# Attention and maxout layer on one Trainium2 core: four units of seven tiles become units of 7, 8, 7 and 6

## The chip, the cores and the metric

The kernel runs on one core of a Trainium2 chip. The metric is the device time of one execution in microseconds; the number given for a kernel is the median of its runs.

## The reference

What is computed, cut to the arithmetic (8 x 8 heads of 576 positions and 64 features, in chunks of 64; the token matrix x is 4608 x 512, d_ff is 768):

```python
scores = scale * np.matmul(q_c, k_c.transpose(0, 1, 2, 4, 3))
scores = scores - np.max(scores, axis=-1, keepdims=True)
attn = np.exp(scores)
attn = attn / (np.sum(attn, axis=-1, keepdims=True) + 1e-09)
out = np.matmul(attn, v_c)
...
x = np.ascontiguousarray(attn_out.transpose(0, 2, 1, 3)).reshape(B * S, H * D)
h = np.maximum(np.maximum(x @ w1, x @ w2), x @ w3)
return (h @ w_out).astype(np.float32)
```

## The kernel before

The 36 tiles of 128 tokens are worked in two groups of four tiles (`GROUPS`) and then in four units of seven (`UNITS`, line 27). For each tile the attention comes first: scores S (L221), the softmax on VectorE, ScalarE and GpSimd (L226 to L188), four transposes T (L244), the values V (L256), and a copy into x. For a group or a unit the hidden layer follows, then the projection with w_out.

Every 32-bit operand is held as a high and a low part, and `three` (L170 to L173) makes of each product three matmuls: low by high, high by low, high by high. In the text a matmul of such a three is called a product.

In the groups the hidden layer is a plain one over 512 tokens. In a unit it is a scheme with seven products for a 2 x 2 block product: the tokens of the unit are two halves of `count * 64` columns (`half`, L404), the d_model is split in two, and pairs of d_ff blocks form the two outputs. `operands` (L434) makes the seven moving operands X1 to X7 from the unit's x in `stage`, as sums and differences of its four blocks. The seven stationary operands, sums and differences of weights, are made once by `store` (L351), written to DRAM and loaded again for each set through a ring of two places (`load`, L440): 768 KB by L443 and 1024 KB by L447. A set is a pair of d_ff blocks and one of w1, w2, w3. There are nine sets in a unit, each with seven products in the order `ORDER = (1, 6, 5, 7, 2, 3, 4)`, each of two halves of the contraction and three matmuls: 42 matmuls a set, 378 a unit, all `half` columns wide. After set n, `load` is planned for set n + 2, into the ring's place that set n has left. Results go from one of five PSUM banks by copies (L471), sums (L474, L477) and GpSimd's sums (L480, L483) into `kept` and `most`, and the maximum over the three weights (L486) is split into the high and low part H (L492, L496). The projection (L521) of a unit runs after its nine sets, 18 matmuls of 512 columns a tile, and its outputs are copied (L518) and stored (L519) through four buffers.

The order on every engine is written out. For the first group it is the string `FIRST`; after it a planner walks through the TensorE steps, keeps a clock `now` by the tabled step times `STEP` (a three with 512 columns) and `STEP_H` (a three of a unit), and puts every other operation into the program when its due time has come. The attention of unit u + 1 is laid into unit u by `tiles` (L689): a *cluster* of V of one tile, S of the tile two further on and T of the next, at equal distances over the time that the caller gives. All of it runs on one stream of TensorE, so a cluster stands between products. Unit 0's tiles are made during the second group; unit 1's from the second group's projection through unit 0's hidden layer; unit 2's from unit 0's projection through unit 1's hidden layer, and so on. The last unit has no attention beside it.

The buffers: `HALF` (line 28) is the width for which `stage`, `kept`, `most` and H are made; X is made 512 wide and cut to `HALF`. `H_AT` (L627) lists the places of the twelve H buffers, six of a pool that the groups used, five of a late pool, one of the attention's.

Of the kernel before, what the change touches and what calls it, by code (L numbers as in the profile page):

```python
# [10 lines left out]
F32R = mybir.dt.float32r  # L11
# [9 lines left out]
P = 128  # L21
NT = B * S // P
DM, DF, DO = 512, 768, 512
CT, JT = DM // P, DF // P
SCALE = 1.0 / float(D) ** 0.5
GROUPS = [4, 4]
UNITS = [7] * 4
HALF = 448
STEP, TILE = 0.6815, 1.55
STEP_H = 0.6003  # L30
ORDER = (1, 6, 5, 7, 2, 3, 4)
SOFTMAX = (("mx", 1.0), ("sub", 1.9), ("exp", 2.8), ("sum", 3.8), ("eps", 4.7), ("rec", 4.9), ("nrm", 5.3))
ON_PE = {"V": 0.6, "S": 0.6, "T": 0.35}
# [29 lines left out]
def chunk_attn_maxout_kernel(  # L63
# [16 lines left out]
    att = ctx.enter_context(tc.tile_pool(name="att", bufs=1))  # L80
# [6 lines left out]
    hpool = ctx.enter_context(tc.tile_pool(name="hpool", bufs=1))  # L87
# [23 lines left out]
    for name in FIRST.split():  # L111
        k = (3 * int(name[1]) + int(name[2])) if name[0] in "WAXY" else None
# [235 lines left out]
    sets = [(jp, w) for jp in range(JT // 2) for w in range(3)]  # L348
# [52 lines left out]
    def unit(t0, count, rooms):  # L401


        half = count * 64  # L404
        X, ring = {}, {}
        hh, hl = [None] * JT, [None] * JT
        stage, m, s = rooms["stage"], rooms["m"], rooms["s"]
# [6 lines left out]
            return lambda: stage()[:, 2 * k:2 * k + 2, c * half:(c + 1) * half]  # L414

        def room(n):
            return lambda: s()[:, 2 * n:2 * n + 2]

        b11, b21, b12, b22 = (block(k, c) for c in range(2) for k in range(2))
        source = {1: b11, 2: b21, 3: b22, 4: room(0), 5: room(0), 6: room(1), 7: b12}  # L420
# [3 lines left out]

        def high(i):
            def fn():
                X[i] = rooms["X"](i)
                nc.scalar.copy(out=X[i][:, 0], in_=source[i]())
            return fn

# [28 lines left out]
        def hidden(n):  # L459
            jp, w = sets[n]  # L460
            a, b = 2 * jp, 2 * jp + 1
            o = {}

            def M(j, c):
                return m()[:, j - a, c, :half]

            def kept(k):
                return s()[:, k, :half]

            def copy(i, k):  # L470
                return lambda: nc.scalar.copy(out=kept(k), in_=o[i])  # L471

            def sum_to(k, i, q):
                return lambda: nc.vector.tensor_tensor(out=kept(k), in0=o[i], in1=kept(q), op=plus)  # L474

            def value(i, k, j, c):
                return lambda: nc.vector.tensor_tensor(out=o[i] if w else M(j, c), in0=o[i], in1=kept(k), op=plus)  # L477

            def third():
                nc.gpsimd.tensor_tensor(out=kept(2), in0=kept(2), in1=kept(1), op=plus)  # L480

            def fourth():
                nc.gpsimd.tensor_tensor(out=kept(1) if w else M(b, 1), in0=kept(1), in1=kept(3), op=plus)  # L483

            def greater(j, c, of):
                return lambda: nc.vector.tensor_tensor(out=M(j, c), in0=of(), in1=M(j, c), op=most)  # L486

            def high(j, c):
                def fn():
                    if hh[j] is None:  # L490
                        hh[j], hl[j] = (rooms["H"](2 * j + k) for k in range(2))
                    nc.scalar.copy(out=hh[j][:, c * half:(c + 1) * half], in_=M(j, c))  # L492
                return fn

            def low(j, c):
                return lambda: nc.vector.tensor_tensor(out=hl[j][:, c * half:(c + 1) * half], in0=M(j, c),  # L496
                                                       in1=hh[j][:, c * half:(c + 1) * half].bitcast(F32), op=minus)

            def most_of(at, j, c, of):
                ops = [(at, greater(j, c, of))] if w else []  # L500
                return ops + ([(at + 1.4, high(j, c)), (at + 2.3, low(j, c))] if w == 2 else [])

            after = {1: [(0.25, copy(1, 0))], 6: [(0.25, sum_to(2, 6, 0))], 5: [(0.25, copy(5, 1))],
                     7: [(0.25, sum_to(3, 7, 2)), (1.0, third), (2.2, fourth)],
                     2: [(0.25, value(2, 0, a, 0))] + most_of(0.8, a, 0, lambda: o[2]),
                     3: [(0.25, value(3, 2, a, 1))] + most_of(0.8, a, 1, lambda: o[3]),
                     4: [(0.25, value(4, 3, b, 0))] + most_of(0.8, b, 0, lambda: o[4]) + most_of(1.4, b, 1, lambda: kept(1))}
            for i in ORDER:
                o[i] = bank()[:, :half]
                for k in range(2):  # L510
                    hi, lo = weights(n, i, k)
                    three(o[i], hi, lo, X[i][:, 0, k, :half], X[i][:, 1, k, :half], k == 0, k == 1)
                    yield STEP_H, after[i] if k else []

        def output(tt, of):
            outputs.append(tt)
# [28 lines left out]
    def hold(name, make):  # L545
        if name not in held:
            held[name] = make()
        return held[name]

    def stage():  # L550
        return hold("stage", lambda: stage_p.tile([P, CT, 2 * HALF], F32, name="stage"))

# [71 lines left out]

    order = []
    late = {}
    H_AT = [(hpool, f"h{k}") for k in range(6)] + [("late", f"k{k}") for k in range(5)] + [(att, "aa")]  # L627

    def H(k):
        pool, tag = H_AT[k]  # L630
        return (late["hold"] if pool == "late" else pool).tile([P, 2 * HALF], F32R, name="H", tag=tag, bufs=1)

    def X(i):
        return hold(("X", i), lambda: late["hold"].tile([P, 2, 2, 512], F32R, name=f"X{i}")[:, :, :, :HALF])

    rooms = dict(
        stage=stage, X=X, H=H,
        m=lambda: hold("m", lambda: late["hold"].tile([P, 2, 2, HALF], F32, name="most")),
        s=lambda: hold("s", lambda: late["hold"].tile([P, 4, HALF], F32, name="kept")),
        ring=lambda n, k: late["hold"].tile([P, (6, 8)[k], 256], F32R, name="ring", tag=f"r{n % 2}{k}"))  # L640

    places = []
    groups, parts = [g0], []
    g = moe(starts[1], lambda: x_tiles(1))
    groups.append(g)
    units, t0 = [], sum(GROUPS)
    for count in UNITS:
        units.append((unit(t0, count, rooms), t0, count))
# [4 lines left out]
    def steps(n):  # L653
        if n not in steps_of:
            t0 = sum(GROUPS)
            first = t0 + n // UNITS[0] * UNITS[0]
            steps_of[n] = begun[t0 + n] if t0 + n in begun else plain_steps(t0 + n, stage, (t0 + n - first) * P)
        return steps_of[n]

    tiles_in_units = sum(UNITS)  # L660

# [13 lines left out]
    def first_tiles(time):  # L675
        gap = (time - 8.0) / 8
        for n in range(UNITS[0] + 2):
            at = now + 7.0 + gap * n
            insert(at, (("V", n - 2), ("S", n)))
            softmax(n, at, nc.vector if n < UNITS[0] else nc.gpsimd)  # L680
            if n < UNITS[0] + 1:
                insert(at + 9.2, (("T", n),))
# [6 lines left out]
    def tiles(u, time):  # L689
        if u >= len(units):  # L690
            return
        lead = 10.9
        gap = (time - 10.0 - lead) / (UNITS[u] - 1)
        for k in range(UNITS[u]):
            n, at = sum(UNITS[:u]) + k, now + lead + gap * k
            insert(at, (("V", n), ("S", n + 2), ("T", n + 1)))
            softmax(n + 2, at, nc.gpsimd)
            plan(at - 16.0, 0.0, lambda n=n: steps(n)["v"]())
            plan(at + 1.0, 0.0, lambda n=n: steps(n)["x"]())
            if n + 1 < tiles_in_units:  # L700
                plan(at + 0.9, 0.0, lambda n=n: steps(n + 1)["at"]())
# [16 lines left out]
    def load(u, n, *at):  # L718
        if n >= len(sets):
            u, n = u + 1, n - len(sets)  # L720
        if u < len(units):
            for t, fn in zip(at, units[u][0]["load"](n)):
                plan(now + t, 0.0, fn)

    inner = 3 * JT * CT * STEP + 7 * TILE
    span = len(sets) * 14 * STEP_H + 6 * TILE
    parts += [("do", lambda: first_tiles(inner - 2.0))]
    parts += [("steps", lambda j=j, w=w: g["hidden"](j, w)) for j in range(JT) for w in range(3)]
    parts += [("do", change), ("do", lambda: operands(0)),
              ("do", lambda: tiles(1, 4 * JT * STEP + span)), ("do", lambda: load(0, 0, 0.0, 1.0)), ("do", lambda: load(0, 1, 2.0, 3.0))]  # L730
    parts += [("steps", lambda: g["project"](0, 1)), ("steps", lambda: g["project"](2)), ("steps", lambda: g["project"](3))]
    for u, (it, t0, count) in enumerate(units):
        for n in range(len(sets)):
            parts.append(("steps", lambda it=it, n=n: it["hidden"](n)))
            parts.append(("do", lambda u=u, n=n: load(u, n + 2, 0.3, 0.9)))
        parts.append(("do", lambda u=u: operands(u + 1)))
        parts.append(("do", lambda u=u, count=count: tiles(u + 2, count * JT * STEP + span + TILE)))
        parts += [("steps", lambda it=it: it["project"](0, 1, 2, before=4))]
        parts += [("steps", lambda it=it, tt=tt: it["project"](tt)) for tt in range(3, count)]
    now = -10.0  # L740
# [8 lines left out]
    with tc.manual_schedule(engines={ET.PE, ET.DVE, ET.Activation, ET.Pool, ET.SP}):  # L749
        first_group()  # L750
        for what, make in parts:
# [3 lines left out]
            for after in make():  # L755
                step, after = after if isinstance(after, tuple) else (STEP, after)
# [36 lines left out]
```

## Time and profile before

| | |
|---|---|
| median of 3 runs | 639.48 us (639.41 to 639.81) |
| the profiled execution | 639.17 us |
| its span in the profile | 637.4 us |
| TensorE busy | 628.0 us |
| VectorE, ScalarE, GpSimd busy | 410.7, 232.7, 214.5 us |
| products of the units, 448 columns | 1512, in four times 378 |
| HBM traffic | 209 GB/s over the span |

The span runs from the first to the last instruction of the program. A row of the timeline has the start, the duration (of merged rows: to the last one's end), the engine, the line, the operation, what it writes and reads, and its size. Durations of TensorE's rows overlap, as matmuls are pipelined; what counts there is the distance between starts. "PE" is TensorE, "PEld" its weight loads, "DVE" VectorE, "ACT" ScalarE, "POOL" GpSimd, "SP" SyncE, which issues the DMAs.

### The profile page before, as it was taken

What the parts mean: (1) busy time and instruction counts of PE and PEld (TensorE: products, weight loads), DVE (VectorE), ACT (ScalarE), POOL (GpSimd) and SP (SyncE); (2) the same over time, 40 slices, a digit from 0 to 9 for tenths busy, and PEclk for the clock granted to TensorE, in tenths of its full rate; (3) what the DMA queues carried; (4) which work ended last, traced back from release to release, by engine and by line L of the source; (5) the groups of instructions that cost most, each with busy time, mean ns of one, the idle gap of its engine ahead of it and who ended that gap; (6) DMA issues with size and microseconds to landing.
All of it is one profiled execution on the core that took longest, in us unless ns stands there. A gap on an engine that the chain in (4) does not pass through costs nothing.

```text
span 637.4 us, 12371 instructions
## 1 busy us (share of the span) xinstructions
PE 628.0 (99%) x5101; PEld 540.8 (85%) x5102; DVE 410.7 (64%) x661; ACT 232.7 (37%) x400; POOL 214.5 (34%) x185
## 2 busy tenths in 40 slices
PE   7899999999999999999999999999999999999997
PEld 3888878878889998888999998898998889999986
DVE  4889854788856676891675769337584842756520
ACT  4888633454532322452132325322331431212121
POOL 2423577765423233231323334023322421222200
PEclk9999999999999999999999999999999999999999
DMA  8988559576846656273466527537563523555211
GB/s 328 358 298 305 184 183 356 212 243 231 316 159 270 248 207 273 79 286 133 173 274 238 220 105 281 198 124 256 216 225 139 214 100 117 201 197 217 111 50 66
DMA packets 35911, 133.70 MB, mean 210 GB/s; under 512 B 3984, under 2 KB 6288, under 8 KB 30096
## 3 DMA queue, kind: packets, MB, share of 16 engines
q1 hardware_dynamic: 35856, 132.92, 56.5%
q8 instruction: 40, 0.66, 0.4%
q14 instruction: 15, 0.12, 0.1%
HBM read 106.95 MB, written 25.95 MB: 209 GB/s over the span
## 4 chain that ended last, share of the span: by engine, by line
PE 91%; DVE 5%; ACT 2%; issue 1%; DVEq 0%; ACTq 0%
PE pm L171 28%; PE pm L172 28%; PE pm L173 28%; PE s L256 3%; PE tp L244 2%; PE s L221 2%; DVE e L231 1%; PE pm L583 1%; DVE mx L226 1%; DVE sm L179 1%; DVE s L382 1%; ACT e L235 1%; DVE sm L182 1%; DVE xl L267 0%; DVE m L307 0%
## 5 line engine op out<-in xcount | busy, mean ns | idle before, releaser
L171 PE MATMUL pm<-X,ring 128*128 128x448 f32 x504 | 185.9, 369 | 0.0
L172 PE MATMUL pm<-X,ring 128*128 128x448 f32 x504 | 184.4, 366 | 0.0
L173 PE MATMUL pm<-X,ring 128*128 128x448 f32 x504 | 184.3, 366 | 0.0
L480 POOL TENSOR_TENSOR kept<-kept 128x448 f32<-128x448 f32 x36 | 41.5, 1153 | 183.2 <-DVE kept L474 148.8
L171 PEld LDWEIGHTS pm<-X,ring 128*128 128x128 f32 x504 | 94.7, 188 | 8.2 <-ACT ao L328 0.4
L173 PEld LDWEIGHTS pm<-X,ring 128*128 128x128 f32 x504 | 94.7, 188 | 7.9
L172 PEld LDWEIGHTS pm<-X,ring 128*128 128x128 f32 x504 | 94.7, 188 | 7.7
L474 DVE TENSOR_TENSOR kept<-pm,kept 128x448 f32<-128x448 f32 x72 | 44.7, 620 | 86.0 <-PE pm L173 86.0
L471 ACT COPY kept<-pm 128x448 f32<-128x448 f32 x72 | 38.2, 533 | 142.7 <-PE pm L173 138.7
L171 PE MATMUL pm<-woh,H 128*128 128x512 f32 x168 | 65.8, 392 | 0.0
L173 PE MATMUL pm<-woh,H 128*128 128x512 f32 x168 | 65.4, 389 | 0.0
L172 PE MATMUL pm<-wol,H 128*128 128x512 f32 x168 | 65.4, 389 | 0.0
L188 POOL TENSOR_TENSOR e<-e,sm 128x512 f32<-128x512 f32 x26 | 27.4, 1053 | 110.8 <-DVE sm L185 105.8
L171 PE MATMUL pm<-xh,wl 128*128 128x512 f32 (+1 forms) x156 | 60.9, 390 | 0.0
L172 PE MATMUL pm<-xl,wh 128*128 128x512 f32 (+1 forms) x156 | 58.4, 375 | 0.3 <-DVE xl L267 0.3
L173 PE MATMUL pm<-xh,wh 128*128 128x512 f32 (+1 forms) x156 | 58.4, 374 | 0.0
L477 DVE TENSOR_TENSOR pm<-pm,kept 128x448 f32<-128x448 f32 x72 | 45.2, 628 | 11.7 <-PE pm L173 10.9
L486 DVE TENSOR_TENSOR most<-pm,most 128x448 f32<-128x448 f32 x72 | 44.9, 623 | 1.9
L226 DVE TENSOR_REDUCE mx<-s 128x8 f32<-128x512 f32 x36 | 24.7, 685 | 32.1 <-PE s L221 32.1
L492 ACT CAST H<-most 128x448 fp32r<-128x448 f32 x48 | 26.8, 568 | 48.3 <-DVE most L486 48.3
L249 ACT COPY xs<-tp 128x512 f32<-128x512 f32 x36 | 21.0, 584 | 50.7 <-PE tp L244 50.6
L173 PEld LDWEIGHTS pm<-woh,H 128*128 128x128 f32 x168 | 31.5, 188 | 6.7
(89 smaller groups left out, 962.4 us busy)
## 6 DMA issues: line engine op xcount, KB each, us to landing
ring<-w SPq DMA_DIRECT2D x36, 1024.0 KB, 6.7
ring<-w SPq DMA_DIRECT2D x36, 768.0 KB, 4.6
buf<-in_qk SPq DMA_DIRECT2D x36, 512.0 KB, 5.9
buf<-in_vb SPq DMA_DIRECT2D x36, 256.0 KB, 5.4
out_x<-ao SPq DMA_DIRECT2D x36, 256.0 KB, 2.1
w<-s SPq DMA_DIRECT2D x9, 1024.0 KB, 5.5
stage<-in_w SPq DMA_DIRECT2D x7, 512.0 KB, 5.2
xl<-in_w SPq DMA_DIRECT2D x5, 512.0 KB, 7.7
```

What stands on the lines that cost most here:

```text
L171: nc.tensor.matmul(out=o, lhsT=al, rhs=bh, start=first, stop=False)
L172: nc.tensor.matmul(out=o, lhsT=ah, rhs=bl, start=False, stop=False)
L173: nc.tensor.matmul(out=o, lhsT=ah, rhs=bh, start=False, stop=last)
L188: eng.tensor_tensor(out=e, in0=e, in1=sm.unsqueeze(2).broadcast_to([P, 8, 64]), op=ALU.mult)
L226: nc.vector.tensor_reduce(out=st["mx"].rearrange("p (g c) -> p c g", c=2), in_=st["s"], axis=AX.X, op=ALU.max)
L249: nc.scalar.copy(out=st["at"], in_=st["tp"])
L471: return lambda: nc.scalar.copy(out=kept(k), in_=o[i])
L474: return lambda: nc.vector.tensor_tensor(out=kept(k), in0=o[i], in1=kept(q), op=plus)
L477: return lambda: nc.vector.tensor_tensor(out=o[i] if w else M(j, c), in0=o[i], in1=kept(k), op=plus)
L480: nc.gpsimd.tensor_tensor(out=kept(2), in0=kept(2), in1=kept(1), op=plus)
L486: return lambda: nc.vector.tensor_tensor(out=M(j, c), in0=of(), in1=M(j, c), op=most)
L492: nc.scalar.copy(out=hh[j][:, c * half:(c + 1) * half], in_=M(j, c))
```

## The change

The four units have 7, 8, 7 and 6 tiles. Their products have 448, 512, 448 and 384 columns; the total of tiles, sets, matmuls and columns stays. `HALF` is 512, and every buffer of a unit has room for 512 columns, of which a unit uses the first `half`. For this two of the H buffers move from the late pool to two attention buffers. The planner's step time depends on the number of tiles, and the functions that used `UNITS[0]` for all units now use each unit's own.

```diff
-UNITS = [7] * 4
-HALF = 448
+UNITS = [7, 8, 7, 6]
+HALF = 512
...
-STEP_H = 0.6003
+STEP_H = {6: 0.52, 7: 0.6003, 8: 0.6815}
...
         def room(n):
-            return lambda: s()[:, 2 * n:2 * n + 2]
+            return lambda: s()[:, 2 * n:2 * n + 2, :half]
...
-                X[i] = rooms["X"](i)
+                X[i] = rooms["X"](i)[:, :, :, :half]
...
-                    yield STEP_H, after[i] if k else []
+                    yield STEP_H[count], after[i] if k else []
...
-    H_AT = [(hpool, f"h{k}") for k in range(6)] + [("late", f"k{k}") for k in range(5)] + [(att, "aa")]
+    H_AT = [(hpool, f"h{k}") for k in range(6)] + [("late", f"k{k}") for k in range(3)] + [(att, k) for k in ("qs", "rv", "aa")]
...
-        return hold(("X", i), lambda: late["hold"].tile([P, 2, 2, 512], F32R, name=f"X{i}")[:, :, :, :HALF])
+        return hold(("X", i), lambda: late["hold"].tile([P, 2, 2, 512], F32R, name=f"X{i}"))
...
-            first = t0 + n // UNITS[0] * UNITS[0]
+            first = t0 + max(sum(UNITS[:u]) for u in range(len(UNITS)) if sum(UNITS[:u]) <= n)
...
-    inner = 3 * JT * CT * STEP + 7 * TILE
-    span = len(sets) * 14 * STEP_H + 6 * TILE
+    inner = 3 * JT * CT * STEP + UNITS[0] * TILE
+    def span(u):
+        return len(sets) * 14 * STEP_H[UNITS[u]] + 6 * TILE
...
-              ("do", lambda: tiles(1, 4 * JT * STEP + span)), ...
+              ("do", lambda: tiles(1, 4 * JT * STEP + span(0))), ...
...
-        parts.append(("do", lambda u=u, count=count: tiles(u + 2, count * JT * STEP + span + TILE)))
+        parts.append(("do", lambda u=u, count=count: tiles(u + 2, count * JT * STEP + span(u + 1) + TILE) if u + 2 < len(units) else None))
```

The program's order moves with it. On TensorE the first cluster inside unit 0's hidden layer stood after 33 products, in the middle of X3's (before; X_2154 is the buffer of X3, `s<-xs,buf` is V, `s<-buf` is S, `tp` is T):

```order
L173 MATMUL pm<-X_2154,ring 128x448
L256 MATMUL s<-xs,buf 64x64 x16
L221 MATMUL s<-buf 64x64 x16
L244 MATMUL tp<-ident,e 128x128 x4
L171 MATMUL pm<-X_2154,ring 128x448
```

After the change, at the same place (X_2166 is the buffer of X7, X_2114 that of X2):

```order
L173 MATMUL pm<-X_2166,ring 128x448
L256 MATMUL s<-xs,buf 64x64 x16
L221 MATMUL s<-buf 64x64 x16
L244 MATMUL tp<-ident,e 128x128 x4
L171 MATMUL pm<-X_2114,ring 128x448
```

It stands after 24 products now, and the clusters behind it follow every 48 or 51 products, where it was 57 or 60. Unit 0's hidden layer holds seven clusters instead of six, unit 1's five as before, unit 2's four instead of five.

On SyncE, in unit 0's projection, the stores of outputs (L519) and the loads of attention inputs (L213 the values, L209 queries and keys), before:

```order
L519 DMA out_x<-ao 128x512
L213 DMA buf<-in_vb 128x512
L519 DMA out_x<-ao 128x512
L209 DMA buf<-in_qk 128x1024
L519 DMA out_x<-ao 128x512 x3
```

After the change:

```order
L519 DMA out_x<-ao 128x512 x2
L213 DMA buf<-in_vb 128x512
L209 DMA buf<-in_qk 128x1024
L519 DMA out_x<-ao 128x512 x4
```

The loads stand together, with more stores behind them. On TensorE in the last unit there is no attention before or after; what changes is the width. Before, its first products are

```order
L171 MATMUL pm<-X_2102,ring 128x448
L172 MATMUL pm<-X_2102,ring 128x448
L173 MATMUL pm<-X_2102,ring 128x448
```

and after the change

```order
L171 MATMUL pm<-X_2102,ring 128x384
L172 MATMUL pm<-X_2102,ring 128x384
L173 MATMUL pm<-X_2102,ring 128x384
```

with 378 of them as before, and 108 matmuls of projection behind them instead of 126.

More of the change, by code (lines that the diff above doesn't have):

```diff
@@ L729, in chunk_attn_maxout_kernel @@
     parts += [("do", change), ("do", lambda: operands(0)),
-              ("do", lambda: tiles(1, 4 * JT * STEP + span)), ("do", lambda: load(0, 0, 0.0, 1.0)), ("do", lambda: load(0, 1, 2.0, 3.0))]
+              ("do", lambda: tiles(1, 4 * JT * STEP + span(0))), ("do", lambda: load(0, 0, 0.0, 1.0)), ("do", lambda: load(0, 1, 2.0, 3.0))]
     parts += [("steps", lambda: g["project"](0, 1)), ("steps", lambda: g["project"](2)), ("steps", lambda: g["project"](3))]
```

## Prediction

> **What bounds the kernel now.** I read the page first, then the busy time by stage, then single instructions of TensorE in the timeline.
>
> The head of the page and its chain:
>
> ```profile
> span 637.4 us, 12371 instructions
> PE 628.0 (99%) x5101; PEld 540.8 (85%) x5102; DVE 410.7 (64%) x661; ACT 232.7 (37%) x400; POOL 214.5 (34%) x185
> PE 91%; DVE 5%; ACT 2%; issue 1%; DVEq 0%; ACTq 0%
> ```
>
> TensorE is busy nearly always, and the chain runs through it. Busy time by stage (columns: stretch, its length, busy us and instructions of each engine, granted clock, DMA share, GB/s); the first three stretches are a unit with its projection, the fourth the last unit's products, the fifth its projection, the sixth the projection of unit 0 alone:
>
> ```profile
> 178.84:298.00 119.16, 119.16 (x1049) 105.26 (x1048) 80.23 (x133) 40.44 (x70) 34.84 (x28) 1.00 0.56 210
> 298.00:415.57 117.57, 117.57 (x981) 104.00 (x980) 75.95 (x126) 37.28 (x65) 33.73 (x27) 1.00 0.55 204
> 415.57:528.39 112.82, 112.82 (x777) 100.00 (x776) 67.33 (x107) 32.47 (x56) 33.64 (x24) 1.00 0.49 182
> 528.39:605.00 76.61, 76.61 (x379) 71.01 (x378) 43.95 (x74) 15.19 (x28) 20.67 (x18) 1.00 0.46 172
> 605.00:633.70 28.70, 28.70 (x127) 23.46 (x125) 4.09 (x8) 5.20 (x9) 0.00 (x0) 1.00 0.14 55
> 266.00:298.00 32.00, 32.00 (x263) 26.33 (x263) 21.49 (x26) 14.03 (x22) 6.95 (x3) 1.00 0.65 239
> ```
>
> In every stage that the change touches TensorE is busy for the whole length at the full granted clock (1.00), so its pace, the distance from one matmul's start to the next one's, sets the time. The duration in a row (0.36 us) overlaps with the next matmul and is no measure. Pairs of starts from the timeline: 256 columns (12 products apart, a row of L171 being every third), 512 columns (93 apart), 448 columns over the whole last unit (378 apart: 9 sets of 42), and 448 columns in another stretch (12 apart).
>
> ```profile
> 29.87 0.28 PE L171 MATMUL pm<-xh,wl 128*128 128x256 f32 x1
> 31.31 0.28 PE L171 MATMUL pm<-xh,wl 128*128 128x256 f32 x1
> ...
> 611.83 0.39 PE L171 MATMUL pm<-woh,H 128*128 128x512 f32 x1
> 632.91 0.39 PE L171 MATMUL pm<-woh,H 128*128 128x512 f32 x1
> ...
> 528.39 0.36 PE L171 MATMUL pm<-X,ring 128*128 128x448 f32 x1
> 605.00 0.39 PE L171 MATMUL pm<-woh,H 128*128 128x512 f32 x1
> ...
> 229.61 0.37 PE L171 MATMUL pm<-X,ring 128*128 128x448 f32 x1
> 232.09 0.37 PE L171 MATMUL pm<-X,ring 128*128 128x448 f32 x1
> ```
>
> The paces are 1.44/12 = 120.0 ns at 256 columns, 21.08/93 = 226.7 ns at 512, 76.61/378 = 202.7 ns at 448 in the last unit and 2.48/12 = 206.7 ns at 448 after 229.6 us. The two clean widths give a line: (226.7 - 120.0)/256 = 0.417 ns a column, and 120.0 - 256 x 0.417 = 13.3 ns beside the columns. At 448 the line says 200.0, and the trace shows 2.7 more, or 6.7 more in some stretches. So 448 is a width at which each product costs a little more than its columns; 256 and 512 are not. The reader is to see that the number of columns stays the same under the change (448 + 512 + 448 + 384 = 4 x 448), so that only such excesses can move the time.
>
> **The change part by part.** Unit 1 gets eight tiles: its 378 products go from 448 to 512 columns. What they take now: the stage from its first product to the first matmul of its projection, less five clusters of score, transpose and value matmuls (counted in the chain), one of which is shown between its neighbours.
>
> ```profile
> 298.00 0.36 PE L171 MATMUL pm<-X,ring 128*128 128x448 f32 x1
> 383.56 0.39 PE L171 MATMUL pm<-woh,H 128*128 128x512 f32 x1
> ...
> 308.74 0.37 PE L173 MATMUL pm<-X,ring 128*128 128x448 f32 x1
> 309.04 0.69 PE L256 MATMUL s<-xs,buf 64*64 64x64 f32 x32
> ...
> 310.83 0.36 PE L172 MATMUL pm<-X,ring 128*128 128x448 f32 x1
> ...
> 278.81 0.39 PE L172 MATMUL pm<-wol,H 128*128 128x512 f32 x1
> 280.42 0.39 PE L173 MATMUL pm<-woh,H 128*128 128x512 f32 x1
> ```
>
> A cluster costs 310.83 - 308.74 = 2.09 us less two products of 0.203, 1.69. So unit 1's products take 85.56 - 5 x 1.69 = 77.1 us, 204.0 ns each, a mixture of the two paces. At 512 they take 378 x 226.7 = 85.7. The last pair shows seven products of 512 columns just after a cluster, 1.61 us instead of 1.59: the pace needs some steps to settle, 0.02 to 0.03 us a cluster, 0.15 with five. New 85.85, which is +8.75 us.
>
> The last unit gets six tiles: 378 products of 384 columns, a width that the trace doesn't show. The line gives 13.3 + 384 x 0.417 = 173.3 ns. Below, I allow 1 ns less. Above, the bound is the excess of 448 at its worst, 180.0. I take 173.3, since both widths that are multiples of 128 lie on the line and 384 is one, 448 not; that this is what matters is a guess from three widths. So 378 x 173.3 = 65.5 us instead of 76.6: -11.1 us. Both units together: **-2.35 us**.
>
> The Trainium skill's TensorE: Matmul & The Clock Gate, Back-to-back issue gap, gives a warm gap of N/2.4 + 2.5 ns, which makes 215.8 and 162.5 ns for 512 and 384, exactly twice the 189.2 for 448: by it the sum would be nought. The trace differs with 226.7 and 202.7 ns, and has at 448 an excess that this rule lacks.
>
> Units 0 and 2 keep 448 columns, but their clusters move: the hidden products of unit 0 have seven instead of six, those of unit 2 four instead of five; the total over the program, and so the clusters' cost, stays. Whether a stretch after a cluster runs at 202.7 or 206.7 I can't foretell: one of some 55 products changing its pace is 0.2 us, and I allow 0.5 both ways.
>
> The projections stay 28 times 18 matmuls; 18 go from the last projection to unit 1's. What follows the last matmul is untouched:
>
> ```profile
> 633.83 0.59 ACT L518 COPY ao<-pm 128x512 f32<-128x512 f32 x1 [3.49 <-PE pm L173]
> 634.44 0.33 SPq L519 DMA_DIRECT2D out_x<-ao  x1
> ```
>
> Evictions and operand splits keep their number and change width. In the last unit VectorE has 43.95 us of work in 76.61; if nothing of it shrank, that would be 67% of 65.5. Its heaviest set (every third: two sums, three values, four maxima, four differences) is 13 operations, and two widths show their size:
>
> ```profile
> L477 DVE TENSOR_TENSOR pm<-pm,kept 128x448 f32<-128x448 f32 x53 | 33.2, 627 | 8.3 <-PE pm L173 8.1
> L231 DVE TENSOR_TENSOR e<-s,mx 128x512 f32<-128x512 f32 x10 | 6.9, 690 | 6.3 <-ACT stage L270 6.3
> ```
>
> 63 ns for 64 columns makes 564 at 384, 13 x 0.564 = 7.3 us in a set of 42 x 0.1733 = 7.28; unshrunk 8.15, a backlog of 0.9, worked off in the next set, which has five operations. What hides it is that five banks leave 4 x 1.04 us before one is needed again. Cost nought; without that cover, up to 0.9 for each of three such sets. Unit 1's operands grow by a seventh in the 32 us around unit 0's projection, where VectorE has 21.5 us of work: nought. The buffers with 512 columns move addresses only: nought.
>
> One tile more in unit 0 brings the clusters 51 or 48 products apart (before 57 to 60). The first comes after 24 products instead of 33, and needs the softmax whose last step is
>
> ```profile
> 181.02 1.04 POOL L188 TENSOR_TENSOR e<-e,sm 128x512 f32<-128x512 f32 x1 [6.96 <-DVE sm L185]
> ```
>
> done at 182.1. The new transpose starts at 178.84 + 24 x 0.203 + about 1.1 = 184.8. So 2.7 us of cover, cost nought. On SyncE's queue in the projections loads of q, k and v now stand ahead of more output stores; the stores have four buffers, and the loads' buffers were freed a cluster or more before. Nought.
>
> Sum: 637.4 - 2.35 = 635.05 span. The profiled execution took 639.17, 1.77 more than its span, so 636.8; the median shown, 639.48, is 0.3 above the profiled one, which makes **637.1 us**.
>
> **The rivals.** *The excess stays with these products* (22%): they may owe it to their operands, not to the width. With 2.7 ns on 512 and 384 the units take 86.7 and 66.5 us, a gain of 0.5; with 384 at 176 alone 1.3, at 180 a loss of 0.2. Time 638.2 to 639.7. For it: all 448-column products are of this kind. Against: in the same stretches the pace jumps between two values, which looks like timing. The page's rule above would land here too, at 639.5.
>
> *Weights arrive late in the six-tile unit* (8%), the slower side. Two sets' weights stand in a ring, and a set's load starts when the set two before is done:
>
> ```profile
> 536.70 0.37 PE L173 MATMUL pm<-X,ring 128*128 128x448 f32 x1
> 537.48 0.42 SPq L447 DMA_DIRECT2D ring<-w  x1
> DMA to landing us min/median/max: 6.3/6.6/6.7
> DMA to landing us min/median/max: 6.3/6.7/11.3
> ```
>
> The first row is the last matmul of a set, the first landing row is of the last unit alone, the second of the whole program. The larger load is issued 0.58 us after the set's end (536.70 plus 0.2) and lands 7.2 after it; it is needed at 7.28 + 6 x 0.173 = 8.3. It decides from a landing of 7.7 us on; at 8.7 each pair of sets loses 1.0 us, 3.5 pairs 3.5 us, 640.6. Against: without attention loads in that unit the longest was 6.7.
>
> The weight loads' own rows (mean of all at 448 columns, then two at 256):
>
> ```profile
> L171 PEld LDWEIGHTS pm<-X,ring 128*128 128x128 f32 x504 | 94.7, 188 | 8.2 <-ACT ao L328 0.4
> 30.11 0.19 PEld L171 LDWEIGHTS pm<-xh,wl 128*128 128x128 f32 x1
> 30.23 0.19 PEld L172 LDWEIGHTS pm<-xl,wh 128*128 128x128 f32 x1
> ```
>
> *Weight loads into the array become the bound* (2%): a load's row lasts 188 ns, more than 173. If they didn't overlap each other, 384 columns would keep 202.7 ns, and the time would be 639.5 + 8.75 + 0 = 648.2. Against: at 256 columns loads of 0.19 us start every 0.12. The Trainium skill's Perfetto Trace Analysis, Identifying the Most-Contended Engine, takes the busy share of weight loads as a measure of how near TensorE is to its limit; that share would pass 100% here, and those two rows say that this is no limit.
>
> *More is gained* (6%): the slow stretches of units 0 and 2 go too, up to 1.0 us, 636.1. That the change doesn't do what it says I leave out: the widths stand in the program.
>
> **How the numbers follow.** My forecast has 62%, 637.1, with its own range 636.2 to 638.0 (0.5 for the clusters, 0.4 for 1 ns of pace). To hold the first rival with its clusters the range goes up to 640.0; the low end stays at 636.2. A difference of 0.2%, 1.28 us, is about what a measurement of this kernel can tell from none. Faster by more: forecast and the larger gain, 0.68. Within: the first rival, 0.22. Slower: late weights and weight loads, 0.10.
>
> **What would show it.** In the new profile the last unit's 378 starts should span 65.5 us (173.3 a step) and unit 1's 85.9 beside its clusters; no wait of TensorE above 0.35 us in the units; weights landing in 6.3 to 6.7 us in the last unit. It is wrong if 384 steps at 176 or more, if 512 doesn't settle at 226.7 with these operands, or if TensorE waits for the ring.

## The result and the profile after

The changed kernel takes 635.74 us (median of 4 runs, 634.9 to 636.14) against 639.44 us before (639.15 to 639.81): ratio 0.995, interval 0.9939 to 0.9962. (The ratios here are those on record. They aren't formed from the two medians, whose quotient is 0.9942; 0.995 stands for 3.2 us.) It is faster, as forecast, and by somewhat more than forecast: 637.1 was predicted, and the median of 635.74 lies 0.5 us under the low end of the range, while the ratio, from the 639.48 that the forecast started from, gives 636.3, just inside it. A second timing (below) gave 636.58 against 638.75, ratio 0.9966, interval 0.9954 to 0.9978, which is 2.2 us and close to the forecast 2.35.

The head of the page after and its chain:

```profile
span 634.3 us, 12373 instructions
PE 624.6 (98%) x5101; PEld 535.2 (84%) x5102; DVE 411.2 (65%) x661; ACT 233.3 (37%) x400; POOL 220.8 (35%) x185
PE 85%; DVE 9%; ACT 2%; issue 2%; DMA 1%; ACTq 0%; DVEq 0%
```

The same stretches as before the change: three units with their projections, the last unit's products, its projection. Columns as before.

```profile
178.48:299.41 120.93, 120.63 (x1118) 106.61 (x1116) 83.21 (x136) 42.18 (x72) 40.03 (x29) 1.00 0.57 214
299.41:429.73 130.32, 130.32 (x1000) 107.36 (x999) 82.82 (x128) 40.58 (x67) 39.36 (x27) 1.00 0.51 186
429.73:540.33 110.60, 110.60 (x710) 98.67 (x709) 63.69 (x102) 30.35 (x53) 31.75 (x23) 1.00 0.48 179
540.33:605.99 65.66, 65.66 (x379) 65.49 (x378) 38.91 (x74) 13.65 (x28) 18.13 (x18) 1.00 0.54 201
605.99:630.63 24.64, 24.64 (x109) 20.09 (x108) 3.76 (x8) 4.48 (x8) 0.00 (x0) 1.00 0.14 54
```

Set against the rows of before, with what the forecast's terms give for each stretch:

| stretch | before | after | difference | forecast |
|---|---|---|---|---|
| up to the first product of unit 0 | 178.84 | 178.48 | -0.36 | 0 |
| unit 0, projection included | 119.16 | 120.93 | +1.77 | +1.69 (a cluster more) |
| unit 1 | 117.57 | 130.32 | +12.75 | +12.83 (8.75, and a projection of 4.08) |
| unit 2 | 112.82 | 110.60 | -2.22 | -1.69 (a cluster less) |
| last unit, products | 76.61 | 65.66 | -10.95 | -11.1 |
| last projection | 28.70 | 24.64 | -4.06 | -4.08 |

The differences sum to -3.07 us, the spans differ by 3.1. The two widths did what the line said. First and last start of unit 1 and of the last unit:

```profile
299.41 0.39 PE L171 MATMUL pm<-X,ring 128*128 128x512 f32 x1
393.66 0.39 PE L171 MATMUL pm<-woh,H 128*128 128x512 f32 x1
...
540.33 0.33 PE L171 MATMUL pm<-X,ring 128*128 128x384 f32 x1
605.99 0.39 PE L171 MATMUL pm<-woh,H 128*128 128x512 f32 x1
```

The last unit steps at 65.66/378 = 173.7 ns, with 0.1 us lost in one place (below), and unit 1 at (94.25 - 5 x 1.69)/378 = 227.0 ns with the settling after its clusters. What the sum didn't have is 0.45 us in units 0 and 2 (0.08 over and 0.53 under the forecast) and the 0.36 us before unit 0. Of these, 0.30 us stand in the idle matmuls at the program's head (last section), which the change doesn't touch: that share is luck of these two executions.

### The profile page after: what moved, and what is told of

Same layout as the page of the kernel before. It is cut to its first block, busy times and chain, and to the rows that moved or that the text cites. A ratio compares the mean times of both kernels' runs of the same rounds, so it can differ in the third digit from the quotient of the medians.

```text
span 634.3 us, 12373 instructions
## 1 busy us (share of the span) xinstructions
PE 624.6 (98%) x5101; PEld 535.2 (84%) x5102; DVE 411.2 (65%) x661; ACT 233.3 (37%) x400; POOL 220.8 (35%) x185
## 4 chain that ended last, share of the span: by engine, by line
PE 85%; DVE 9%; ACT 2%; issue 2%; DMA 1%; ACTq 0%; DVEq 0%
PE pm L171 26%; PE pm L172 26%; PE pm L173 26%; PE s L256 2%; PE tp L244 2%; PE s L221 2%; DVE X L432 1%; DVE s L382 1%; DVE e L231 1%; DVE mx L226 1%; DVE sm L179 1%; PE pm L583 1%; DMA w<-s 1%; DVE sm L182 1%; DVE kept L423 1%
## 5 line engine op out<-in xcount | busy, mean ns | idle before, releaser
L171 PE MATMUL pm<-X,ring 128*128 128x448 f32 (+2 forms) x504 | 184.8, 367 | 0.3 <-ACT ao L328 0.3
L172 PE MATMUL pm<-X,ring 128*128 128x448 f32 (+2 forms) x504 | 183.2, 363 | 0.0
L173 PE MATMUL pm<-X,ring 128*128 128x448 f32 (+2 forms) x504 | 183.2, 363 | 0.0
L480 POOL TENSOR_TENSOR kept<-kept 128x448 f32<-128x448 f32 (+2 forms) x36 | 41.5, 1152 | 180.6 <-DVE kept L474 145.8
L474 DVE TENSOR_TENSOR kept<-pm,kept 128x448 f32<-128x448 f32 (+2 forms) x72 | 44.7, 621 | 80.5 <-PE pm L173 80.2
L471 ACT COPY kept<-pm 128x448 f32<-128x448 f32 (+2 forms) x72 | 38.3, 532 | 149.2 <-PE pm L173 144.2
L477 DVE TENSOR_TENSOR pm<-pm,kept 128x448 f32<-128x448 f32 (+2 forms) x72 | 45.2, 628 | 11.6 <-PE pm L173 11.6
L486 DVE TENSOR_TENSOR most<-pm,most 128x448 f32<-128x448 f32 (+2 forms) x72 | 44.9, 623 | 2.0
L492 ACT CAST H<-most 128x448 fp32r<-128x448 f32 (+2 forms) x48 | 27.2, 569 | 49.3 <-DVE most L486 49.3
L231 DVE TENSOR_TENSOR e<-s,mx 128x512 f32<-128x512 f32 x36 | 24.8, 690 | 19.0 <-ACT stage L270 18.8
```

The lines of the kernel that those rows point to most:

```text
L171: nc.tensor.matmul(out=o, lhsT=al, rhs=bh, start=first, stop=False)
L172: nc.tensor.matmul(out=o, lhsT=ah, rhs=bl, start=False, stop=False)
L173: nc.tensor.matmul(out=o, lhsT=ah, rhs=bh, start=False, stop=last)
L231: nc.vector.tensor_tensor(out=st["e"].rearrange("p g c k -> p c g k"), in0=st["s"], in1=most.unsqueeze(3).broadcast_to([P, 2, 4, 64]), op= ...
```

## The experiments

**Theory:** the time follows the pace of the matmuls, and at 448 columns that pace has an excess which 512 and 384 lack; the rest of the gain is that no stretch of units 0 and 2 runs at 206.7 ns any more. **Rivals:** the wider rooms and other addresses bring it, the clusters' number and place bring it, or what else the expectations name.

**The rooms alone.** The new code with four units of seven:

```diff
-UNITS = [7, 8, 7, 6]
+UNITS = [7] * 4
```

> The new code and rooms for 512 columns, with four units of seven. Theory (the gain comes from the widths 512 and 384 alone): nothing is gained, 639.4 us, 638.8 to 640.0 with the slow stretches at 206.7 ns falling otherwise; all unit products step at 202.7 or 206.7 ns. Rival (the other buffers or addresses bring it): 635.7 to 637.5 us.

Measured: 638.68 us against 638.93, ratio 0.9994 (0.9984 to 1.0003). Its stretches are those of before to 0.1 us. So rooms and addresses are not the cause.

**No unit at 448 columns, the first try.**

```diff
-UNITS = [7, 8, 7, 6]
+UNITS = [8, 8, 6, 6]
...
-        gap = (time - 8.0) / 8
+        gap = (time - 8.0) / (UNITS[0] + 1)
```

> Units of 8, 8, 6 and 6 (the spacing of the first unit's tiles is divided by nine instead of eight). Theory: no unit is left at 448 columns, so products take 2 x 85.7 + 2 x 65.5 = 302.4 us instead of 304.4 in the changed kernel, 2.0 us less, 633.7 us, steps 226.7 and 173.3 ns. Rival (the gain of the changed kernel came from fewer or better placed clusters): 635.7 us or more, as the clusters are as many.

Measured: 640.24 us, ratio 1.0021 (1.001 to 1.0032), slower than before. The steps are 226.7 and 173.3 ns as expected, but the first product of unit 0 starts at 183.96 us instead of 178.48. TensorE's waits between 120 and 190 us of this kernel (waiting line, releaser, us, times, longest):

```profile
PE s L256 <- ACT xs L249: 4.2, 4, 1.9
PE pm L171 <- ACT ao L328: 1.1, 1, 1.1
```

The attention of eight tiles doesn't fit beside the second group: the value matmuls wait for the copies of their transposes. My expectation had the pace and not the place where a first unit's tiles are made. By its time alone this run falls on the rival's side, at 635.7 us or more; what speaks for the theory are the steps, and that the loss stands in these waits. The next run leaves them out.

**The same widths with a light first unit.**

```diff
-UNITS = [7, 8, 7, 6]
+UNITS = [6, 8, 8, 6]
...
-        gap = (time - 8.0) / 8
+        gap = (time - 8.0) / (UNITS[0] + 1)
```

> Units of 6, 8, 8 and 6 (the spacing of the first unit's tiles is divided by seven instead of eight): no unit at 448 columns, and a lighter first unit, whose tiles are made beside the second group. Theory (pace of widths, and the loss of units 8, 8, 6, 6 came from TensorE waiting for the eight tiles beside the second group): products 2 x 65.6 + 2 x 85.85 = 302.9 us instead of 304.7 in the changed kernel, 1.8 us less than it, ratio to before 0.9923, no wait before 178 us beyond those of the changed kernel. Rival (denser attention beside the smaller unit costs TensorE as much as it did with 8, 8, 6, 6): not faster than the changed kernel, 0.995 or above.

It ran beside the changed kernel itself:

> The changed kernel as it is, timed beside the kernel before on the chip that runs the next two. Forecast's theory with the stretches at 206.7 ns of units 0 and 2 gone: 3.1 us less than before, ratio 0.995. If the first measurement was lucky by more than its clusters: 0.9963.

Measured: 636.58 us for the changed kernel, ratio 0.9966 (0.9954 to 0.9978), and 634.75 us for units of 6, 8, 8 and 6, ratio 0.9936 (0.9923 to 0.9948), both against 638.75. The difference of the two is 1.83 us, where 1.8 was expected from 302.9 and 304.7 us of products. That it agrees to 0.03 us is luck, since this kernel also loses 0.8 us to a wait (below). The profiles say it without head and projections: the four hidden layers, less 1.69 us for each cluster with transposes in them, take 308.2 us before, 305.5 in both profiles of the changed kernel and 303.2 with 6, 8, 8 and 6. The changed kernel's gain is smaller than at first: the two intervals overlap (0.9954 to 0.9962), but each ratio lies outside the other's interval, and 0.9963, the expectation for a lucky first measurement, lies inside the second. The last unit's products with 6, 8, 8 and 6 are those of the changed kernel:

```profile
539.04:604.64 65.60, 65.60 (x379) 65.49 (x378) 38.91 (x74) 13.67 (x28) 18.14 (x18) 1.00 0.54 201
```

**Late weights, provoked.**

```diff
-UNITS = [7, 8, 7, 6]
-STEP_H = {6: 0.52, 7: 0.6003, 8: 0.6815}
+UNITS = [8, 8, 8, 4]
+STEP_H = {4: 0.36, 6: 0.52, 7: 0.6003, 8: 0.6815}
...
-        gap = (time - 8.0) / 8
+        gap = (time - 8.0) / (UNITS[0] + 1)
```

> Units of 8, 8, 8 and 4: the last unit's products have 256 columns. By the line of paces alone (3 x 85.7 + 378 x 0.120 = 302.4 us) it would be as fast as units of 8, 8, 6 and 6, 633.7 us. Theory of the ring: a set lasts 5.04 us there, its weights land 7.2 us after the set two before and are needed at 5.04 + 6 x 0.12 = 5.8, so TensorE waits 1.4 us or more a pair of sets, 5 us in all, 638.7 us, with waits of TensorE for the ring in the last unit.

Measured: 647.7 us in one run. Unit 0 starts at 184.77 us, 6.3 us later than in the changed kernel, as it did by 5.5 us with 8, 8, 6 and 6; 1.7 us of this is a cluster that now stands there and no longer in a unit. In the last unit TensorE waits for the ring, as expected:

```profile
PE pm L171 <- DMA ring<-w: 5.2, 5, 1.7
PE pm L171 <- DVE most L486: 0.5, 1, 0.5
```

Its products take 52.6 us (573.28 to 625.84) where 378 x 0.120 = 45.4 would do, 7.2 us more where 5 were expected. All of it stands at the seventh and eighth products of sets, where the larger load is first read; the 5.2 us of the view are the part in which TensorE is idle. In the changed kernel the same mechanism only just shows. Landing times of the larger load in its last unit, and the one place where the pace breaks there:

```profile
DMA to landing us min/median/max: 6.3/6.5/7.6
...
570.34 0.34 PE L173 MATMUL pm<-X,ring 128*128 128x384 f32 x1
570.55 0.41 PE L171 MATMUL pm<-X,ring 128*128 128x384 f32 x1
570.80 0.34 PE L172 MATMUL pm<-X,ring 128*128 128x384 f32 x1
```

The step after 570.34 is the seventh of a set, the first that reads the larger load; it comes 0.04 us late and the next 0.08. One load landed in 7.6 us, outside the 6.3 to 6.7 that the forecast named and just short of its point of 7.7; the cost is 0.1 us. It isn't always so small: the second profile of the changed kernel has no such step, the last unit of the last kernel below loses 0.4 us at one, with a longest landing of 7.9.

**The pace over the width.** Columns of the products of w2 are cut in each unit, and what is cut is left out of the computation:

```diff
+WIDTHS = {8: (440, 432, 416), 15: (400, 424, 446), 22: (368, 352, 320), 28: (480, 496, 448)}
...
+            cut = WIDTHS[t0][jp] if w == 1 else half
...
-                o[i] = bank()[:, :half]
+                o[i] = bank()[:, :cut]
...
-                    three(o[i], hi, lo, X[i][:, 0, k, :half], X[i][:, 1, k, :half], k == 0, k == 1)
+                    three(o[i], hi, lo, X[i][:, 0, k, :cut], X[i][:, 1, k, :cut], k == 0, k == 1)
```

> Units of 7, 7, 6 and 8, and in each unit the three sets of w2 work on fewer columns than the unit has, the rest of these columns being left out: 440, 432, 416; 400, 424, 446; 368, 352, 320; 480, 496, 448. Only the steps between starts are read. Line: 13.3 ns + 0.417 ns a column, so 146.7 at 320, 160.0 at 352, 166.7 at 368, 180.0 at 400, 186.7 at 416, 190.0 at 424, 193.3 at 432, 196.7 at 440, 199.2 at 446, 213.3 at 480, 220.0 at 496. Theory A (only multiples of 128 are clean): all of these lie 1 to 7 ns above the line. Theory B (only something near 448 is not clean): 320 to 432 and 480 lie on the line within 1 ns, 440 to 448 above it. 320 tells whether odd multiples of 64 are it (then 2.7 or 6.7 above), 448 stands there as a control with 202.7 or 206.7 in a unit that is 512 wide.

Four sets without a cluster, the first start and the start of the next set, 42 products each (400, 480, 496 and 448 columns, the last inside a 512-column unit; the lines' numbers are one higher here):

```profile
305.33 0.34 PE L172 MATMUL pm<-X,ring 128*128 128x400 f32 x1
312.90 0.36 PE L172 MATMUL pm<-X,ring 128*128 128x448 f32 x1
...
518.81 0.38 PE L172 MATMUL pm<-X,ring 128*128 128x480 f32 x1
527.91 0.39 PE L172 MATMUL pm<-X,ring 128*128 128x512 f32 x1
...
546.95 0.38 PE L172 MATMUL pm<-X,ring 128*128 128x496 f32 x1
556.19 0.39 PE L172 MATMUL pm<-X,ring 128*128 128x512 f32 x1
...
575.23 0.36 PE L172 MATMUL pm<-X,ring 128*128 128x448 f32 x1
583.74 0.39 PE L172 MATMUL pm<-X,ring 128*128 128x512 f32 x1
```

They give 180.2, 216.7, 220.0 and 202.6 ns, against 180.0, 213.3, 220.0 and 200.0 of the line. Means over all steps of a width that no cluster or wait stands in:

| columns | 320 | 352 | 368 | 384 | 400 | 416 | 424 | 432 | 440 | 446 | 448 | 480 | 496 | 512 |
|---|---|---|---|---|---|---|---|---|---|---|---|---|---|---|
| step, ns | 146.3 | 161.1 | 166.6 | 173.9 | 180.1 | 188.4 | 193.2 | 195.8 | 200.0 | 200.2 | 203.6 | 216.7 | 220.0 | 226.7 |
| over the line | -0.3 | 1.1 | -0.1 | 0.6 | 0.1 | 1.7 | 3.2 | 2.5 | 3.4 | 1.1 | 3.6 | 3.4 | 0.0 | 0.1 |

Neither theory A nor theory B holds. 320, 368, 400 and 496 are clean and no multiples of 128, and 480 is not clean and far from 448. A part of it can be named afterwards: 424, 440 and 446, the three widths that are no multiples of 16, step within 0.2 ns as the line says of the next multiple (193.3 at 432, 200.0 at 448). For the excess at 352, 416, 432, 448 and 480 I can name no rule in the number of columns. Each cut width stands in a single set of one unit, so that a second pace, as 448 has it, isn't excluded for the others. The excess belongs to the width and not to the operands of a unit: 448 has it inside a 512-column unit, 512 with the same operands has none.

**The slow stretches at 448.** In the traces of before and after, the steps at 448 run in a cycle of five. These rows of before stand ahead of a cluster that throws TensorE into the slow stretch from 228.6 us on:

```profile
225.68 0.36 PE L172 MATMUL pm<-X,ring 128*128 128x448 f32 x1
225.88 0.36 PE L173 MATMUL pm<-X,ring 128*128 128x448 f32 x1
226.08 0.37 PE L171 MATMUL pm<-X,ring 128*128 128x448 f32 x1
226.29 0.36 PE L172 MATMUL pm<-X,ring 128*128 128x448 f32 x1
226.49 0.37 PE L173 MATMUL pm<-X,ring 128*128 128x448 f32 x1
226.79 0.69 PE L256 MATMUL s<-xs,buf 64*64 64x64 f32 x32
```

To the nanosecond the steps that end at the fourth and fifth of them are 207 and 202, behind a 199. Every cluster of S, T and V that starts at this point of the cycle, five in before, is followed by a slow stretch, and none that starts elsewhere. So the kernel before was changed in its clusters alone:

```diff
-        lead = 10.9
-        gap = (time - 10.0 - lead) / (UNITS[u] - 1)
+        lead = 10.9 if u == 1 else 9.7
+        gap = 20 * STEP_H + TILE if u == 1 else 25 * STEP_H + TILE
```

> The kernel before, four units of seven, with the clusters of attention laid so that each stands after 60 or 75 products of the stretch before (first ones after 33 and 57) instead of 54, 57, 60, 69 or 72. Theory (at 448 columns the steps run in a cycle of five, 199, 207, 202, 203, 202 ns, and a cluster that starts behind its third step throws TensorE into the steady 206.7 ns): no stretch at 206.7 ns, where before has five of 60 to 72 products, so 1.4 us less than before, ratio 0.9978. Rival (which stretch is slow doesn't hang on the place in the cycle): as many slow stretches, ratio 1.000.

Measured: 639.27 us, ratio 1.0004 (0.9995 to 1.0013): no gain. Yet no stretch at 206.7 ns is left, and the products of units 0, 1 and 2 take 86.86, 85.01 and 83.69 us instead of 87.17, 85.56 and 84.25, 1.4 us less. It was given back in one place, in unit 1's projection:

```profile
390.44 0.39 PE L173 MATMUL pm<-woh,H 128*128 128x512 f32 x1
392.21 0.50 PE L171 MATMUL pm<-woh,H 128*128 128x512 f32 x1 [1.39 <-DVE H L496]
```

The step of 1.77 us instead of 0.23 is a new wait: VectorE was late with H, and the projection's first step that reads it waited. The wider spacing had put a tile's attention beside the unit's last set, which was taken for the cause. So the clusters were laid closer:

```diff
-        gap = (time - 10.0 - lead) / (UNITS[u] - 1)
+        gap = 20 * STEP_H + TILE
```

> The kernel before, four units of seven, with the clusters 60 products apart in all units and the first one 33 products into a unit, so that none starts behind the third step of the cycle of five and none stands near a unit's end, where the run before this lost 1.5 us to a wait for H. Theory: no stretch at 206.7 ns and no new wait of TensorE above 0.4 us, 1.4 us less than before, ratio 0.9978. Rival (the slow stretches' 1.4 us are given back elsewhere whatever the place of the clusters): ratio 1.000.

Measured: 637.8 us against 638.53, ratio 0.9983 (0.9974 to 0.9991), 1.1 us less by the ratio and 0.7 between the medians. There is no slow stretch and no wait in the units, which take 86.82, 85.01 and 83.68 us. The theory is confirmed; the forecast 0.9978 lies in the interval.

**The wait that 6, 8, 8 and 6 have left.** They lose 0.8 us at 386.8 us, in unit 1's projection, to H. From that kernel:

```diff
-        gap = (time - 10.0 - lead) / (UNITS[u] - 1)
+        gap = (time - 16.0 - lead) / (UNITS[u] - 1)
```

> Units of 6, 8, 8 and 6 with the clusters closer together, so that they end earlier in each unit. Theory (the 0.8 us wait of the first projection step that follows unit 1's products comes from the attention's VectorE work beside that unit's last set): that wait and the 0.2 us one in unit 0's projection go, 0.8 to 1.0 us less than with the wider spacing, ratio to before 0.9923. Rival (VectorE is late there by its own 512-column work): same ratio as with the wider spacing, 0.9936, and the wait stays.

Measured: 634.4 us, ratio 0.9934 (0.9921 to 0.9947): the rival's outcome came, the wait stays. But VectorE's own work, the rival's reason, is not the whole of it. GpSimd and VectorE at that place:

```profile
384.33 3.31 POOL L423 TENSOR_TENSOR stage<-stage 128x1024 f32<-128x1024 f32 x1 [6.06 <-DVE kept L423]
...
385.31 3.48 DVE L496 TENSOR_TENSOR H<-most,H 128x512 fp32r<-128x512 f32 x2
```

Two operations of VectorE that take 0.68 us each elsewhere need 3.48 us, while GpSimd makes the next unit's operand over 1024 columns. GpSimd is done at 387.64 us, and VectorE's two end at 388.79, 1.15 us later, about what the two need in a row: the first stood until GpSimd was done. The Trainium skill's SBUF — State Buffer, Who interferes with whom, says that an operation of VectorE with two inputs in SBUF contends with a GpSimd operation that reads SBUF; these rows agree. The two profiles of the changed kernel, one and the same program, show it both ways at this place of unit 0's projection, the first profile ahead of the second:

```profile
272.76 6.65 POOL L423 TENSOR_TENSOR stage<-stage 128x1024 f32<-128x1024 f32 x1 [5.64 <-DVE kept L423]
273.73 1.16 DVE L496 TENSOR_TENSOR H<-most,H 128x448 fp32r<-128x448 f32 x2
...
272.98 3.31 POOL L423 TENSOR_TENSOR stage<-stage 128x1024 f32<-128x1024 f32 x1 [5.64 <-DVE kept L423]
273.95 3.35 DVE L496 TENSOR_TENSOR H<-most,H 128x448 fp32r<-128x448 f32 x2
```

In the first GpSimd needs twice its time and VectorE none extra, and TensorE doesn't wait for H; in the second it is VectorE that needs longer, and TensorE waits. This wait, the one of 1.39 us above and those of both kernels with 6, 8, 8 and 6 each end less than 0.1 us after such a held-up operation. Without GpSimd's operation it wasn't tried.

## Why the prediction came out as it did

**Right, to the second digit: the pace.** 384 columns at 173.3 (173.7 with one late load), 512 with a unit's operands at 226.7, +8.69 and -10.95 us for the two stages where +8.75 and -11.1 were forecast. The experiments back that this is the cause: the rooms alone give nothing, and with the two last units of 448 columns moved to clean widths the hidden layers take 2.3 us less again, where the same sum gives 1.8 (0.3 of the rest is the changed kernel's first wait, below).

**Right for a wrong reason: why 384 is clean.** The three multiples of 128 that were measured are clean. But 320, 368, 400 and 496 are clean too, so being such a multiple, which the forecast guessed to be the reason, isn't what matters. A width such as 424 or 440 would have had 3.2 or 3.4 ns over the line; that 384 has none was luck as well as reading.

**Too small: units 0 and 2.** I had them at nought with 0.5 either way, since I couldn't foretell the slow stretches. Before has one in unit 0 and two in unit 2, 60, 72 and 72 products at 4.0 ns more, 0.8 us; the first profile after has none, the second only 17 products behind the wait at unit 0's start. This is what the rival *more is gained* had, with 6% and up to 1.0 us: the result is the forecast's pace with this rival's term added. It could have been foretold: the trace of before shows at which step of the cycle each cluster starts, and the order shows where the clusters go. The later kernels show that in all units together such stretches cost 1.4 us in the profile, 1.1 as timed.

**Missing: two small waits.** In unit 0 the seventh product comes late:

```profile
179.49 0.36 PE L173 MATMUL pm<-X,ring 128*128 128x448 f32 x1
180.16 0.47 PE L171 MATMUL pm<-X,ring 128*128 128x448 f32 x1 [0.30 <-ACT ao L328]
```

That step takes 0.66 us, before 0.35, for a bank that the output copy still had; 0.3 us. And the cover of unit 1's wider operands was counted as enough, by VectorE's work alone; in the second profile of the changed kernel unit 0's projection waits 0.33 us for H at 276.3 us, in the first not at all, by which of VectorE and GpSimd was held up (above). Both waits are small, and the forecast had put both at nought.

**The rivals.** The excess didn't stay with the products (496, 400 and 512 have none). The late weights exist, but cost 0.1 us or nothing in the changed kernel, and 7.2 us at 256 columns, where the arithmetic of landing and need said 5. The weight loads into the array are no bound: 378 loads of 188 ns, 71 us together, go into 65.66 us, one every 174 ns. By the linear rule of the Trainium skill's TensorE: Matmul & The Clock Gate, Back-to-back issue gap, the sum was nought; the measured steps differ from N/2.4 + 2.5 ns by 10.9 ns at 512 and by 13 to 18 at 448, and it is the uneven part of this that the change lives on.

**The range.** 635.74 is under it, by an amount that the kernel's own runs spread over (634.9 to 636.14, and 635.54 to 637.87 in the second timing). The range was made of the clusters and the pace and left this spread out; the head (below) may be a part of it.

The fastest version tried is units of 6, 8, 8 and 6: 634.75 and 634.4 us, 4.0 to 4.1 us under before.

## What to carry to other kernels

Where TensorE is never idle, measure the distance between matmul starts for each width and compare it with a line through the other widths: an excess of a few ns is worth microseconds over a thousand matmuls, and equal numbers of columns aren't equal times. A uniform split isn't the best one by itself; but look where each piece's preparation is made, since the first, bigger piece cost 5 us beside work that had no room for it. A gain on the stream's pace is easily given back by one late operand at a stage's end, so read the waits after moving anything, and look there for work of VectorE and GpSimd that stands in each other's way.

## What the runs showed of the hardware that was not expected

At 448 columns the steps follow a cycle of five (199, 207, 202, 203, 202 ns, mean 202.7) or stand at 206.7, and which of the two is set by the step at which other matmuls, or a wait, cut in. 480 columns alternate between 212 and 221 ns. 496 stands at 220 in all its steps.

The head of the program varies from run to run. Its 13 idle matmuls take 5.73 us in the profile of before, 5.42 in that of the changed kernel and 4.30 with 8, 8, 6 and 6, though they are the same in all kernels; in order (idle matmuls work on zeros, and nobody reads their results):

```profile
1.46 5.73 PE L583 MATMUL pm<-h 128*128 128x512 bf16 x13 [1.46 <-DVE h L585]
...
1.45 5.42 PE L583 MATMUL pm<-h 128*128 128x512 bf16 x13 [1.45 <-DVE h L585]
...
1.46 4.30 PE L583 MATMUL pm<-h 128*128 128x512 bf16 x13 [1.46 <-DVE h L585]
```

The steps in them are 427 or 216 ns, and what varies is how many are slow. Over all profiles the first useful matmul starts between 5.69 and 7.11 us. In the changed kernel, the one program with two profiles, it starts at 6.81 and 6.94 us, so how much of the spread between runs of one program is made here stays open. The Trainium skill's TensorE: Matmul & The Clock Gate, Part 1, says that the clock is halved until a window of activity is over, and that the window doesn't start with the kernel; the steps agree with that, as 427 is close to twice 216; the granted clock stands at 1.00 in these stretches and doesn't show it, and the window itself no run here shows.
